# Attention and expert layer on one core: scores of both heads of a pair made at once on halves of TensorE's rows

## The chip, the cores and the metric

The kernel runs on one core of a Trainium2 chip. The metric is the device time of one execution in microseconds (us); the time before the change is the median of three runs, 732.33 us (732.0 to 733.63).

## The reference, cut to what matters

```python
# q, k, v: (8, 8, 576, 64) float32; w_gate (512,), w1 (512, 1024), w2 (1024, 512); capacity 128
q_rot, k_rot = rotate(q), rotate(k)      # halves x1, x2: x1*cos - x2*sin, x1*sin + x2*cos
scores = 0.125 * q_rot @ k_rot.T         # for each batch and head, 576 x 576
attn = exp(scores - max(scores)); attn = attn / (sum(attn) + 1e-9)
x = attn @ v                             # heads side by side: (8, 576, 512)
for b in range(8):
    s = x[b] @ w_gate                    # one score for each token
    top = the 128 tokens with the largest s
    y = relu(x[b, top] @ w1) @ w2
    out[b] = x[b]; out[b, top] += y / (1 + exp(-s[top]))[:, None]
```

Inputs and outputs are float32.

## The kernel before, in words

**Pairs and units.** The work is cut into 32 pairs of heads, four for each batch. A pair has 576 query rows for each of two heads: four tiles of 128 rows for each head (units 0 to 7, the head is the unit's last bit) and the last 64 rows of both heads together (unit 8). Partition p of a main tile holds tokens 4p to 4p+3, so the 64 left over are the "rem" rows.

**From q and k to operands.** `load` brings q, k and v of a pair with DMAs on SyncE (SP). `rotate` makes the rotation on GpSimd (POOL), for the first pair on VectorE (DVE) in two halves. `turn_qk` turns tiles on TensorE (PE) with transposes against an identity and evacuates them from PSUM with ScalarE (ACT) and DVE. The operands of the scores are float32r, and values are split into a high part and a rest. Before the change a stack of 128 rows held one head: `rotate` writes k twice side by side, so that a turned tile has k on both halves of the partitions; q is written as high part and rest side by side. `k1` is the high part of k, `k2` the rest, and one product of 128 rows gives (qh + ql) times kh, a second (qh + ql) times kl: four terms with two products, each for 576 columns in two pieces of 288. That makes 18 transposes a pair: 9 of k in float32 (L418), 9 of q in float32r (L421).

**Scores and softmax.** `unit` (L506) makes the scores of one unit, four matmuls (eight for unit 8) of 288 columns at L519, into one of two score tiles of PSUM (`s_ps`, two banks each). Then DVE takes the row maximum (L532), and ACT the exponential with its sum (L536), which frees the score tile. `turn` (L562) and `turn_rem` (L577, L580) transpose the attention weights, ACT or DVE copy them out (the helper at L232 and L234), and `value` (L612) multiplies them with v: the two heads of a pair stand on the two column halves of the array, 64 columns each. The result is turned back (L633), scaled (L643), and a half row of the output is stored and multiplied with the gate's weights.

**Route and experts.** After the last pair of a batch `route` ranks the 576 gate scores with comparisons on DVE (L752, L760), finds the 128 chosen tokens, gathers them with an indirect DMA, and `experts_of` runs the two layers on them (L872) while the next batch's attention goes on. The experts of the last but one batch are held back to fill the wait for the last batch's route. The expert weights come in 16 DMAs through two staging tiles, and are split by ACT (L933) and POOL (L935), in the first tens of microseconds.

**What sets the order.** Every step is an operation with the engines it can run on, an assumed duration, the operations that it needs and a key. `Order.run` (L61) goes through time once while the program is built and gives each engine that is free the ready operation with the smallest key; that fixes the order on every engine's queue. On the chip each engine works through its queue in that order and waits for what an instruction needs. `KEY` holds the offsets of the keys. PSUM has four more tiles of one bank (`t_ps`) for all else. Steps that cost PE a change of the array's tiling (`mode`) are charged 92 ns in the planner's count.

Of the kernel before, what the change touches and what calls it, by code (L numbers as in the profile page):

```python
# [22 lines left out]
KEY = dict(ahead=5800, lag=5900, rem=0, value=6200, rows=6000, load=117900, rotate=29000, half=7100, gate=29300,  # L23
           route=31600, count=35100, select=13200, turn=53900, step=4600, kstep=1200, hold=3)


class Bank:


    def __init__(self, kind):  # L30
        self.kind, self.slot, self.left, self.end = kind, None, 0, 0.0


class Op:
    __slots__ = ("engines", "fn", "key", "bank", "waits", "outs", "ready", "start", "end", "done", "mode", "seq")


class Order:

# [7 lines left out]
    def op(self, engines, fn, key, after=(), bank=None, mode=0):  # L47

        o = Op()
        o.engines, o.fn, o.key, o.bank, o.mode = engines, fn, key, bank, mode  # L50
# [5 lines left out]
        if bank is not None:  # L56
            bank.left += 1
        self.ops.append(o)
        return o

    def run(self):  # L61
# [18 lines left out]
        while events:  # L80
# [4 lines left out]
            while moved:  # L85
                moved = False
                for e in names:
                    if free[e] > t:
                        continue
                    put, found = [], None  # L90
                    while waiting[e]:
# [4 lines left out]
                        fits = o.ready <= t  # L96
                        if fits and o.bank is not None and o.bank.slot is None:
                            fits = any(a <= t for a, _ in banks[o.bank.kind])
                        if fits:
                            found = o  # L100
                            break
# [3 lines left out]
                    if found is None:  # L105
                        continue
# [11 lines left out]
                    b = o.bank  # L118
                    if b is not None and b.slot is None:
                        ready = min(x for x in banks[b.kind] if x[0] <= t)  # L120
                        banks[b.kind].remove(ready)
                        b.slot = ready[1]
# [4 lines left out]
                    if b is not None:  # L127
                        b.left -= 1
                        b.end = max(b.end, o.end)
                        if not b.left:  # L130
# [33 lines left out]
def attention_moe_kernel(ctx: ExitStack, tc: tile.TileContext, q, k, v, w_gate, w1, w2, rope, outs, cap):  # L164
# [14 lines left out]

    nc = tc.nc  # L180
# [11 lines left out]
    NS = 2 * NT + 1  # L192
# [15 lines left out]
    order = Order({"s": len(s_banks), "t": len(t_banks)})  # L208
# [27 lines left out]
    def bank_of(b):  # L236
        return (s_banks if b.kind == "s" else t_banks)[b.slot]
# [4 lines left out]
    ident_r = sb("ident_r", [P, P], F32R)  # L242
    nc.vector.tensor_copy(ident_r, ident)
    tabs = sb("tabs", [P, 2, NS, D])
# [5 lines left out]
    q_ins = ring("q_in", 2, [P, NS, D])  # L250
    k_ins = ring("k_in", 2, [P, NS, D])
    m2s = ring("m2", 1, [P, NS, D])
    rks = ring("rk", 1, [P, NS, 2, D])
    rqs = ring("rq", 1, [P, NS, 2, D], F32R)
    k1s = ring("k1", 2, [P, 2, KW], F32R)
    k2s = ring("k2", 2, [P, 2, KW], F32R)
    q1s = ring("q1", 2, [P, 2, 512], F32R)
    qrs = ring("qr", 2, [P, 2, 192], F32R)
# [27 lines left out]
    rjs = ring("rj", 1, [P, S], BF16)  # L286
# [3 lines left out]
    for t_ in qrs.tiles:  # L290
        nc.vector.memset(t_.bitcast(F32)[:, 0, 64:192], 0.0)
# [37 lines left out]
    def load(pi):  # L329
# [12 lines left out]
        for n, src, use, late in (("k", k, kin, 0), ("q", q, qin, 1)):  # L342
            dst = use.tile
            dma(n, dst[:, 0:2 * NT, :].rearrange("p (h t) d -> p h t d", h=2), main(src), use, late)
            for h in range(2):
                dma(n, dst[h * 64:h * 64 + 64, 2 * NT, :], rem(src, h), use, late)
# [5 lines left out]
    def rotate(pi):  # L352
# [5 lines left out]
        parts = ((0, NT), (NT, NS)) if first else ((0, NS),)  # L358
        made = {"k": [], "q": []}
# [11 lines left out]
        for s0, s1 in parts:  # L371
            ss, ns = slice(s0, s1), s1 - s0
            cos, sin = tabs[:, 0, ss], tabs[:, 1, ss]
            for name, use, n_ in (("k", kin, 1), ("q", qin, 0)):
                x, m = use.tile[:, ss], m2.tile[:, ss]
                ms = []
                for w in range(2):
                    ws, wo = slice(32 * w, 32 * w + 32), slice(32 - 32 * w, 64 - 32 * w)
                    ms.append(tt(ns * 32, m[:, :, ws], x[:, :, wo], sin[:, :, ws], ALU.mult,
                                 got[name] + m2.before + m2.users + wait, [m2, use]))  # L380
                y = tt(ns * D, x, x, cos, ALU.mult, ms, [use])
                if n_:
                    r = rk.tile[:, ss]
                    yy, mm = (t_.unsqueeze(2).to_broadcast([P, ns, 2, D]) for t_ in (x, m))
                    o = tt(ns * D * 2, r, yy, mm, ALU.add, [y] + rk.before, [use, m2, rk])
                    made["k"].append((s0, o))
                else:
                    hi, lo = rq.tile[:, ss, 0], rq.tile[:, ss, 1]
                    if first:
                        a = tt(ns * D, x, x, m, ALU.add, [y], [use, m2])  # L390
                        h = op({"ACT": act(ns * D)}, lambda hi=hi, x=x: nc.scalar.copy(hi, x), key, [a])
                        rq.by(h)
# [607 lines left out]
```

## Time and profile before

| | before |
|---|---|
| median of three runs | 732.33 us |
| the profiled execution's own time | 733.43 us |
| its span | 731.7 us |
| granted TensorE clock, mean | 0.995 |
| PE busy | 691.9 us, 95% |
| DVE busy | 520.7 us, 71% |
| POOL busy | 490.3 us, 67% |
| ACT busy | 479.6 us, 66% |
| chain that ended last | PE 80%, DVE 6%, issue 5%, ACT 4% |

How to read it: the span runs from the first to the last instruction of the profiled execution, and 1.7 us of its own time lie outside the span. Matmuls are pipelined, so a matmul's recorded duration holds its whole way through the array: what a matmul costs TensorE is the distance to the next start, not its duration. A group's row has its instructions, their summed and mean duration, and behind the bar the idle time of the engine just before them with what ended it.

### The profile page before, as it was taken

What the parts mean: (1) busy time and instruction counts of PE and PEld (TensorE: products, weight loads), DVE (VectorE), ACT (ScalarE), POOL (GpSimd) and SP (SyncE); (2) the same over time, 40 slices, a digit from 0 to 9 for tenths busy, and PEclk for the clock granted to TensorE, in tenths of its full rate; (3) what the DMA queues carried; (4) which work ended last, traced back from release to release, by engine and by line L of the source; (5) the groups of instructions that cost most, each with busy time, mean ns of one, the idle gap of its engine ahead of it and who ended that gap; (6) DMA issues with size and microseconds to landing.
All of it is one profiled execution on the core that took longest, in us unless ns stands there. A gap on an engine that the chain in (4) does not pass through costs nothing.

```text
span 731.7 us, 14829 instructions
## 1 busy us (share of the span) xinstructions
PE 691.9 (95%) x5200; PEld 571.8 (78%) x5200; DVE 520.7 (71%) x1373; ACT 479.6 (66%) x1155; POOL 490.3 (67%) x446
## 2 busy tenths in 40 slices
PE   3789899999999999999999999999999999999986
PEld 2777688788878887888878878788878888788665
DVE  5466568987897478974788658984789747886551
ACT  2777667677777577765777658775777657776311
POOL 3799999878786488773875768864887648741101
PEclk9999999999999999999999999999999999999989
DMA  5334322122212122121312112121221112000100
GB/s 173 108 108 123 94 64 81 49 71 76 80 51 67 33 79 82 50 63 50 96 48 68 50 54 74 49 82 34 78 82 51 49 54 90 17 24 11 50 26 30
DMA packets 55146, 47.95 MB, mean 66 GB/s; under 512 B 17952, under 2 KB 51744, under 8 KB 55072
## 3 DMA queue, kind: packets, MB, share of 16 engines
q1 hardware_dynamic: 53648, 42.23, 19.4%
q0 software_dynamic: 1280, 4.20, 1.7%
q8 instruction: 41, 0.67, 0.4%
q10 hardware_dynamic: 144, 0.59, 0.3%
q14 instruction: 33, 0.27, 0.1%
HBM read 35.45 MB, written 11.53 MB: 64 GB/s over the span
## 4 chain that ended last, share of the span: by engine, by line
PE 80%; DVE 6%; issue 5%; ACT 4%; DMA 2%; POOL 1%; SPq 0%; POOLq 0%; ACTq 0%; DVEq 0%
PE s_ps L519 22%; PE t_ps L612 21%; PE t_ps L562 16%; PE t_ps L872 9%; PE t_ps L418 4%; PE t_ps L421 3%; PE t_ps L633 2%; ACT pab L536 2%; DVE rj L760 2%; PE t_ps L577 2%; DVE rj L752 1%; PE t_ps L580 1%; PE t_ps L891 1%; DMA k_in<-k_dram 1%; ACT pt L232 1%
## 5 line engine op out<-in xcount | busy, mean ns | idle before, releaser
L532 DVE TENSOR_REDUCE nm<-s_ps 128x1 f32<-128x576 f32 x288 | 215.0, 750 | 94.3 <-PE s_ps L519 85.2
L536 ACT ACTIVATE pab<-s_ps,nm 128x576 f32<-128x576 f32 x256 | 192.5, 752 | 38.6 <-DVE nm L532 37.2
L519 PE MATMUL s_ps<-k,q 128*128 128x288 f32 x1024 | 200.0, 318 | 8.7 <-ACT pab L536 8.5
L519 PEld LDWEIGHTS s_ps<-k,q 128*128 128x128 f32 x1024 | 147.2, 191 | 30.1 <-issue 12.8
L232 ACT COPY pt<-t_ps 128x512 f32<-128x512 f32 x214 | 126.4, 591 | 60.7 <-PE t_ps L562 56.9
L562 PE MATMUL t_ps<-ident,pab 128*128 128x128 f32 x1024 | 155.1, 274 | 8.5 <-DVE rj L760 5.8
L612 PE MATMUL t_ps<-pt,vt 128*64 128x320 f32 (+1 forms) x1024 | 139.0, 412 | 0.3 <-ACT pk L232 0.2
L562 PEld LDWEIGHTS t_ps<-ident,pab 128*128 128x128 f32 x1024 | 122.9, 141 | 16.8 <-ACT pt L232 7.2
L366 POOL TENSOR_TENSOR rk<-k_in,m 128x1152 f32<-128x1152 f32 x31 | 82.0, 2646 | 73.0 <-PE t_ps L418 72.7
L612 PEld LDWEIGHTS t_ps<-pt,vt 128*64 128x64 f32 x1024 | 69.0, 136 | 48.2 <-issue 5.0
L234 DVE COPY pt<-t_ps 128x512 f32<-128x512 f32 x74 | 50.7, 685 | 26.6 <-PE t_ps L562 19.7
L232 ACT COPY ot<-t_ps 128x320 f32<-128x320 f32 (+1 forms) x63 | 25.2, 400 | 61.5 <-PE t_ps L612 61.5
L705 POOL TENSOR_TENSOR prod<-x,wg 128x512 f32<-128x512 f32 (+1 forms) x45 | 49.3, 1096 | 19.4 <-DVE gp L710 18.9
L911 POOL DMA_INDIRECT out_dram<-xe,idx x7 | 7.4, 1054 | 80.0 <-DVE xe L907 80.0
L418 PE MATMUL t_ps<-ident,rk 128*128 128x128 f32 x288 | 48.0, 278 | 9.0 <-DVE rk L366 9.0
L366 POOL TENSOR_TENSOR m<-k_in,tabs 128x288 f32<-128x288 f32 x62 | 49.0, 809 | 10.9 <-DVE q_in L366 10.9
L872 PE MATMUL t_ps<-w,ht 128*128 128x512 f32 x192 | 53.3, 419 | 0.0
L536 ACT ACTIVATION_READ_ACCUMULATOR pab<-s_ps,nm 128x1 f32 x256 | 52.9, 207 | 0.0
L872 PE MATMUL t_ps<-w,xt 128*128 128x512 f32 x192 | 49.9, 400 | 0.0
L432 ACT CAST k<-t_ps 128x512 fp32r<-128x512 f32 x64 | 38.0, 596 | 17.8 <-PE t_ps L418 17.0
L366 POOL TENSOR_TENSOR m<-q_in,tabs 128x288 f32<-128x288 f32 x62 | 48.6, 803 | 1.2
L434 DVE TENSOR_TENSOR k<-t_ps,k 128x512 fp32r<-128x512 f32 x64 | 43.4, 680 | 7.3 <-ACT k L432 7.3
(120 smaller groups left out, 1158.2 us busy)
## 6 DMA issues: line engine op xcount, KB each, us to landing
k_in<-k_dram SPq DMA_DIRECT2D x32, 256.0 KB, 2.7
q_in<-q_dram SPq DMA_DIRECT2D x32, 256.0 KB, 2.8
vt<-v_dram SPq DMA_DIRECT2D x32, 256.0 KB, 2.7
out_dram<-x SPq DMA_DIRECT2D x16, 512.0 KB, 3.5
xe<-w_dram SPq DMA_DIRECT2D x8, 256.0 KB, 2.8
row<-w_dram SPq DMA_DIRECT2D x8, 256.0 KB, 2.7
k_in<-k_dram SPq DMA_DIRECT2D x64, 16.0 KB, 2.3
q_in<-q_dram SPq DMA_DIRECT2D x64, 16.0 KB, 2.4
```

Source lines behind the costliest of these rows:

```text
L232: nc.scalar.copy(out, in_)
L234: nc.vector.tensor_copy(out, in_)
L366: lambda: e.tensor_tensor(out, in0, in1, op=alu), key, after)
L418: nc.tensor.transpose(out, rk.tile[:, i].rearrange("p s d -> p (s d)"), ident)
L434: lambda: nc.vector.tensor_tensor(lo, bank_of(b), hi.bitcast(F32), op=ALU.subtract),
L519: nc.tensor.matmul(bank_of(b)[:, n, 0:HALF], lt, rt[:, n * HALF:n * HALF + HALF], start=(i == 0), stop=(i == len(mms) - 1),)
L532: lambda: nc.vector.tensor_reduce(nm.tile[:, u:u + 1], bank_of(b)[:, :, 0:HALF], axis=AX.XY, op=ALU.max, negate=True),
L536: lambda: nc.scalar.activation(dst.rearrange("p (n c) -> p n c", n=2), bank_of(b)[:, :, 0:HALF], AF.Exp, bias=nm.tile[:, u:u + 1], scale=1 ...
L562: nc.tensor.transpose(bank_of(b)[:, kt * P:kt * P + P], src.tile[:, col + kt * P:col + kt * P + P], ident)
L612: nc.tensor.matmul(bank_of(acc)[hp, 0:n], lt, rt, start=kt == 0, stop=kt == NT)
L705: lambda t0=t0, t1=t1, n=n, prod=prod: nc.gpsimd.tensor_tensor(prod.tile[0:n, 0:t1 - t0], x.tile[0:n, t0:t1, :], wg[0:n, cs].unsqueeze(1). ...
L872: nc.tensor.matmul(bank_of(bank), lhs.tile[:, a, c * P:c * P + P], w[w_][:, c, fs], start=(c == 0 and i == 0), stop=(c == n - 1 and i == 2))
```

## The change

q and k are packed by pair: after `rotate` a tile has head 0 on columns 0 to 63 and head 1 on columns 64 to 127, so that turned tiles hold head 0 on partitions 0 to 63 and head 1 on partitions 64 to 127. `turn_qk` then turns 5 tiles of k and 5 of q, all in float32, and splits each into high part and rest (`kh`, `kl`, `qh`, `ql`). `units` makes the scores of one tile of both heads in one operation: twelve matmuls of 288 columns that alternate between partitions 0 to 63 (head 0, score tile a) and 64 to 127 (head 1, score tile b), for the three terms qh kh, qh kl and ql kh; the fourth, ql kl, is left out. Unit 8 keeps all 128 rows (the other head's rows of q are zero) and has 6 matmuls in score tile a. Such an operation needs both score tiles at once. The planner has a new rule: an engine doesn't start an operation when an operation marked urgent (scores, maximum, exponential) can start within 900 ns (`patience`), unless it ends at most 400 ns (`over`) behind that. The keys of all steps, the layout of the rotation's tables and a scratch tile of `route` change too. The rotation of the first pair is no longer cut in two, and its ACT casts (L391) are gone. k's rem rows come with one DMA where there were two.

```diff
+           gate=11700, route=58400, count=35500, select=12400, turn=17500, step=7600, kstep=2700, hold=3,
+           patience=900, over=400)
...
+                        can = o.ready
+                        for b in o.banks:
+                            if b.slot is None:
+                                can = max(can, min((a for a, _ in banks[b.kind]), default=1e12))
+                            elif b.last != e:
+                                can = max(can, b.free)
+                        if can > t:
+                            if o.urgent and can < t + KEY["patience"] and (soon is None or can < soon):
+                                soon = can
+                        elif soon is None or t + o.engines[e][0] <= soon + KEY["over"]:
                             found = o
...
-                        begin += 92.0 * (o.mode != mode) + 70.0 * (t > free[e] + 1)
+                        begin += 97.0 * (o.mode != mode) + 70.0 * (t > free[e] + 1)
...
-    order = Order({"s": len(s_banks), "t": len(t_banks)})
+    order = Order({"a": 1, "b": 1, "t": len(t_banks)})
...
-                    yy, mm = (t_.unsqueeze(2).to_broadcast([P, ns, 2, D]) for t_ in (x, m))
-                    o = tt(ns * D * 2, r, yy, mm, ALU.add, [y] + rk.before, [use, m2, rk])
+            by_head = lambda t_: t_[:, 0:2 * NT].rearrange("p (h t) d -> p h t d", h=2)
+            o = [tt(2 * NT * D, r.tile[:, 0:NT].rearrange("p t h d -> p h t d"), by_head(x), by_head(m), ALU.add,
+                    [y] + r.before, [use, m2, r])]
...
+        kb, ko = turned([(rk, t) for t in range(NT)], base, made["k"][0:1])
+        k_main = split(kb, ko, base, 512, kh.tile[:, REM:REM + 512], kl.tile[:, REM:REM + 512],
+                       lambda: bank_of(kb), 1.0, kh, kl)
...
+        rb, ro = turned([(rk, NT), (rq, NT)], key, made["k"][1:] + made["q"][1:])
...
+        qb, qo = turned([(rq, t) for t in range(NT)], key, made["q"][0:1])
+        q_main = split(qb, qo, key, 512, qh.tile[:, 0:512], ql.tile[:, 0:512],
+                       lambda: bank_of(qb), D ** -0.5, qh, ql)
...
+    STARTS = {(0, 1): 0, (2, 3): 2, (4, 5): 4, (8,): 6, (6, 7): 7}
...
+            bs = tuple(Bank("ab"[i]) for i in range(len(us)))
             mms = []
+            for a, b in ((qh, kh), (qh, kl), (ql, kh)):
+                for n in range(2):
+                    for i, u in enumerate(us):
+                        hp = slice(64 * i, 64 * i + 64) if u < 8 else slice(0, P)
+                        c0, k0 = (u // 2 * P, REM - REM * i) if u < 8 else (512, REM)
+                        mms.append((i, n, a is qh and b is kh, a is ql, a.tile[hp, c0:c0 + P],
+                                    b.tile[hp, k0 + n * HALF:k0 + n * HALF + HALF]))
...
-            o = op(pe(2 * len(mms) * M288), products, key, needs, b)
+            o = op(pe(6 * (M288 + 6 * (len(us) - 1))), products, key, have + room + (q_rem if us[0] == 8 else []), bs,
+                   mode=2 * (len(us) - 1), urgent=True)
```

The lines of the changed program that the rows below name: L428 transposes of k and q, L494 scores, L540, L555 and L558 transposes of the attention weights, L590 value products, L611 transposes of the output, L354 loads, L906 and L911 gate and expert weights, L912 the casts of the expert weights, L438 and L441 the high parts of k and q, L515 the exponentials. Buffers are named with their number: `s_ps0` and `s_ps1` are the two score tiles (a and b).

**TensorE, the second pair's first score units.** Before the change these rows stand there; `q11` and `k11` are the second pair's operands, `vt0` the first pair's v.

```order
L612 MATMUL t_ps3_68<-pk10_110,vr0_99 64x320 x2
L519 MATMUL s_ps1_64<-k11_89,q11_93 128x288 x2
L519 MATMUL s_ps1_64<-k21_91,q11_93 128x288 x2
L519 MATMUL s_ps0_63<-k11_89,q11_93 128x288 x2
L519 MATMUL s_ps0_63<-k21_91,q11_93 128x288 x2
L633 MATMUL t_ps2_67<-ident_69,ot10_112 128x128 x3
```

In the changed program the same place reads so; a group of scores has twelve rows, of which the first two and the last are shown.

```order
L494 MATMUL s_ps0_63<-kh1_87,qh1_91 128x288
L494 MATMUL s_ps1_64<-kh1_87,qh1_91 128x288
...
L494 MATMUL s_ps1_64<-kh1_87,ql1_93 128x288
L540 MATMUL t_ps1_66<-ident_69,pab3_103 128x128 x4
L555 MATMUL t_ps2_67<-ident_69,pab2_102 128x128
L555 MATMUL t_ps2_67<-ident_69,pab3_103 128x128
L558 MATMUL t_ps2_67<-ident_69,pr0_104 128x128 x2
L428 MATMUL t_ps3_68<-ident_69,rk0_84 128x128 x4
L540 MATMUL t_ps0_65<-ident_69,pab0_100 128x128 x4
```

Two units now stand in one block that alternates between both score tiles, and before the next block there are only transposes, 16 here: the block behind them needs both tiles again.

**SyncE, the loads at the start.** Before the change the expert weights' first DMA (`xe0`) stands behind v of the third pair (`vt2`) and a reload of `k_in0`.

```order
L338 DMA vr1_100<-v_dram 64x64 x2
L338 DMA vt2_98<-v_dram 128x2x256
L338 DMA vr2_101<-v_dram 64x64 x2
L338 DMA k_in0_83<-k_dram 128x2x256
L338 DMA k_in0_83<-k_dram 64x64 x2
L927 DMA wg_77<-w_gate_dram 128x512
L932 DMA xe0_128<-w1_dram 128x512
```

In the changed program it follows the loads of the first two pairs.

```order
L354 DMA vr1_98<-v_dram 64x64 x2
L906 DMA wg_75<-w_gate_dram 128x512
L911 DMA xe0_126<-w1_dram 128x512
L911 DMA row0_128<-w1_dram 128x512
L354 DMA k_in0_81<-k_dram 128x2x256
```

Six DMAs have moved behind the first two weight loads, and k's rem rows are one DMA each.

**ScalarE, the first exponentials.** Before the change one weight cast (`w1_0`) stands ahead of them.

```order
L478 ACTIVATE qr0_94<-t_ps3_68 128x2x64
L448 ACTIVATE q10_92<-t_ps0_65 128x512
L933 CAST w1_0_142<-xe0_128 128x512
L536 ACTIVATE pab0_102,sums0_115<-s_ps0_63,nm0_118 128x576
L536 ACTIVATE pab0_102,sums0_115<-s_ps1_64,nm0_118 128x576
```

In the changed program two do.

```order
L441 ACTIVATE qh0_90<-t_ps2_67 128x128
L912 CAST w1_0_139<-xe0_126 128x512
L912 CAST w1_0_139<-row0_128 128x512
L515 ACTIVATE pab0_100,sums0_113<-s_ps0_63,nm0_116 128x576
L515 ACTIVATE pab0_100,sums0_113<-s_ps1_64,nm0_116 128x576
```

So the first exponentials wait for two weight loads instead of one, and these loads are issued earlier.

More of the change, by code (lines that the diff above doesn't have):

```diff
@@ L20 @@
 EPS = 1e-9
-KEY = dict(ahead=5800, lag=5900, rem=0, value=6200, rows=6000, load=117900, rotate=29000, half=7100, gate=29300,
-           route=31600, count=35100, select=13200, turn=53900, step=4600, kstep=1200, hold=3)
+KEY = dict(ahead=8500, lag=13000, rem=400, value=4300, rows=18600, load=22300, rotate=115700, half=2500,
+           gate=11700, route=58400, count=35500, select=12400, turn=17500, step=7600, kstep=2700, hold=3,
+           patience=900, over=400)
 class Bank:
     def __init__(self, kind):
-        self.kind, self.slot, self.left, self.end = kind, None, 0, 0.0
+        self.kind, self.slot, self.left, self.end, self.last, self.free = kind, None, 0, 0.0, None, 0.0
 class Op:
-    __slots__ = ("engines", "fn", "key", "bank", "waits", "outs", "ready", "start", "end", "done", "mode", "seq")
+    __slots__ = ("engines", "fn", "key", "banks", "waits", "outs", "ready", "start", "end", "done", "mode", "seq", "urgent")
 class Order:
@@ L55, in op @@
             a.outs.append(o)
-        if bank is not None:
-            bank.left += 1
+        for b in banks:
+            b.left += 1
         self.ops.append(o)
@@ L126, in run @@
                     heapq.heappush(events, free[e])
-                    if b is not None:
+                    for b in o.banks:
                         b.left -= 1
                         b.end = max(b.end, o.end)
+                        b.last, b.free = e, b.end + self.SEM
+                        heapq.heappush(events, b.free)
                         if not b.left:
@@ L420, in q_turn, with turned @@
-        def q_turn(out, i):
-            nc.tensor.transpose(out, rq.tile[:, i].rearrange("p s d -> p (s d)"), ident_r)
-        def k_main(h, key):
+        def turned(tiles, key, needs):
             b = Bank("t")
             def turns():
-                for t in range(NT):
-                    k_turn(bank_of(b)[:, t * P:t * P + P], h * NT + t)
-            hi, lo = k1.tile[:, h, REM:REM + 512], k2.tile[:, h, REM:REM + 512]
-            o = op(pe(4 * T32), turns, key, by("k", h * NT), b)
-            c = op({"ACT": act(512)}, lambda: nc.scalar.copy(hi, bank_of(b)), key, [o] + k1.before, b)
-            d = op({"DVE": dve(512)},
-                   lambda: nc.vector.tensor_tensor(lo, bank_of(b), hi.bitcast(F32), op=ALU.subtract),
-                   key, [c] + k2.before, b)
-            rk.by(o), k1.by(c, d), k2.by(d)
-            have[f"k{h}"] += [c, d]
@@ L484, in turn_qk @@
-        step = KEY["kstep"]
-        k_main(0, base)
-        q_main(0, base + step)
-        rems(base + 2 * step)
-        k_main(1, base + 3 * step)
-        q_main(1, base + 4 * step)
-        stacks[pi] = (q1, qr, k1, k2, have)
+                for i, (r, t) in enumerate(tiles):
+                    nc.tensor.transpose(
+                        bank_of(b)[:, i * P:i * P + P], r.tile[:, t].rearrange("p h d -> p (h d)"), ident)
+            o = op(pe(len(tiles) * T32), turns, key, needs + kh.before + kl.before + qh.before + ql.before, b)
```

248 lines of the change are left out of this document (108 added, 140 removed).

## The prediction

> **What bounds the kernel now.** I read the page's busy times first, then the stages, TensorE's waits, and a stretch of TensorE's timeline for prices.
>
> ```profile
> PE 691.9 (95%) x5200; PEld 571.8 (78%) x5200; DVE 520.7 (71%) x1373; ACT 479.6 (66%) x1155; POOL 490.3 (67%) x446
> ```
>
> Busy TensorE may only be a pipeline full of latency, so the stages must confirm it. Two successive batches in the middle (columns: window, its length, then busy time of PE, PEld, DVE, ACT, POOL with instructions, TensorE's clock, DMA):
>
> ```profile
> 203.30:289.10 85.80, 84.74 (x653) 70.47 (x651) 63.54 (x166) 59.03 (x144) 60.46 (x54) 1.00 0.21 63
> 289.10:374.80 85.70, 84.63 (x652) 70.38 (x651) 63.46 (x166) 58.93 (x144) 60.41 (x54) 1.00 0.21 62
> ```
>
> A batch takes 85.7 us, and TensorE is idle for 1.1 of them, at full clock; DVE has 22 us to spare, ACT 27, POOL 25. What TensorE waits for in the whole span (sum, times, longest):
>
> ```profile
> PE t_ps L418 <- DVE rk L366: 9.0, 2, 7.9
> PE s_ps L519 <- ACT pab L536: 8.6, 13, 4.0
> PE t_ps L562 <- DVE rj L760: 5.8, 7, 0.8
> ...
> PE t_ps L562 <- ACT pab L536: 2.7, 3, 1.1
> ```
>
> The 9.0 are the first rotation, the 5.8 the route of each batch. TensorE's work sets the time, so I price the change as work of TensorE, then ask which wait takes the place of that work. A stretch of TensorE (start, length, operation):
>
> ```profile
> 300.32 0.60 PE L562 MATMUL t_ps<-ident,pab 128*128 128x128 f32 x4
> 300.85 2.37 PE L612 MATMUL t_ps<-pt,vt 128*64 128x320 f32 x16
> 303.06 0.71 PE L612 MATMUL t_ps<-pk,vr 128*64 128x320 f32 x4
> 303.69 0.80 PE L519 MATMUL s_ps<-k,q 128*128 128x288 f32 x4
> 304.33 0.60 PE L562 MATMUL t_ps<-ident,pab 128*128 128x128 f32 x4
> 304.68 0.77 PE L519 MATMUL s_ps<-k,q 128*128 128x288 f32 x4
> 305.29 0.60 PE L562 MATMUL t_ps<-ident,pab 128*128 128x128 f32 x4
> 305.73 0.60 PE L844 MATMUL t_ps<-ident,xe 128*128 128x128 f32 x4
> 306.17 0.60 PE L418 MATMUL t_ps<-ident,rk 128*128 128x128 f32 x4
> 306.52 0.54 PE L421 MATMUL t_ps<-ident_r,rq 128*128 128x128 f32 x4
> 306.99 0.80 PE L519 MATMUL s_ps<-k,q 128*128 128x288 f32 x4
> 307.62 0.60 PE L562 MATMUL t_ps<-ident,pab 128*128 128x128 f32 x4
> 307.98 1.30 PE L519 MATMUL s_ps<-k,qr 128*128 128x288 f32 x8
> 309.11 0.38 PE L577 MATMUL t_ps<-ident,pab 128*128 128x128 f32 x2
> ```
>
> Starts give the prices. Four float32 transposes take 0.44 us (305.29 to 305.73 to 306.17): 0.109 each. Eight score matmuls run from 307.62 + 0.44 = 308.06 to 309.11: 0.132 each. Four float32r transposes run from 306.17 + 0.44 = 306.61 to 306.99: 0.095 each.
>
> The same rows price a change of the array's tiling. Transposes end at 300.32 + 0.44 = 300.76, the value product on column halves starts at 300.85: 0.09 us of nothing. On the way out its last two pairs need 2 x 0.27 from 303.06, so 303.60, and scores start at 303.69: 0.09 again. And the first unit behind it takes 0.64 (303.69 to 304.33) where one behind transposes takes 305.29 - (304.33 + 0.44) = 0.52: 0.11 us in which the first weights load with nothing over them.
>
> **The change part by part.** Counts and durations of the groups:
>
> ```profile
> L519 PE MATMUL s_ps<-k,q 128*128 128x288 f32 x1024 | 200.0, 318 | 8.7 <-ACT pab L536 8.5 <-DVE k L472 0.2
> L519 PE MATMUL s_ps<-k,qr 128*128 128x288 f32 x256 | 41.8, 305 | 0.2 <-ACT pab L536 0.2
> L612 PE MATMUL t_ps<-pt,vt 128*64 128x320 f32 x512 | 76.7, 439 | 0.3 <-ACT pk L232 0.2
> L612 PE MATMUL t_ps<-pt,vt 128*64 128x256 f32 x512 | 62.3, 385 | 0.0
> L418 PE MATMUL t_ps<-ident,rk 128*128 128x128 f32 x288 | 48.0, 278 | 9.0 <-DVE rk L366 9.0
> L421 PE MATMUL t_ps<-ident_r,rq 128*128 128x128 f32 x288 | 42.4, 262 | 3.3 <-DVE rq L366 3.3
> ```
>
> *Scores.* Before: 1280 matmuls x 0.132 = 169.0 us. After, for each pair, 4 groups of 6 slots with two matmuls each (one a half of rows), and 6 full matmuls for unit 8. What is a slot worth? No row shows halves of rows; the nearest are the halves of columns. There 64 columns more make a matmul 439 - 385 = 54 ns longer, 0.84 ns a column, so 320 columns stream for 0.27 us; yet 16 matmuls start within 2.21 us (300.85 to 303.06), 0.14 each. So two run at once, at almost no cost. Bounds for a slot of scores: 0.132 (the second matmul free) and 0.264 (one after the other). I take 0.139, near the value product's behaviour. Sum: 768 x 0.139 + 192 x 0.132 = 132.1, a gain of 36.9 us.
>
> The Trainium skill's "TensorE: Matmul & The Clock Gate" (Measured speedup vs the span model) has four row tiles 3.07 times as fast, 77% of four. By that rule a slot is 0.264 / 1.53 = 0.172, an estimate, and the gain on scores only 11.6.
>
> *Transposes of q and k.* Before 288 x 0.109 + 288 x 0.095 = 58.8 us, after 320 x 0.109 = 34.9: a gain of 23.9.
>
> *Changes of tiling.* Every group on row halves stands between work in another tiling. The order of the changed program has 327 changes on TensorE, the order before 128 (64 value products, in and out). Into a score group: 0.09 + 0.11 = 0.20, 128 times, 25.6 us. Into a value product: 0.09 + about 0.05 for its half as wide weights, 64 times, 9.0. Back to transposes or full matmuls: 0.09 and a first load that these rows bound by 0 and 0.11, I take 0.07, 135 times, 21.6. Together 56, before 20 by the same prices (64 x 0.14 and 64 x 0.18): a loss of 36. This eats the whole gain on scores.
>
> *The start.* The first scores of before stand behind the rotation, and then behind a weight load:
>
> ```profile
> 16.16 2.25 PE L519 MATMUL s_ps<-k,q 128*128 128x288 f32 x8
> ...
> 20.98 0.62 ACT L933 CAST w<-xe 128x512 fp32r<-128x512 f32 x1 [3.98 <-DMA xe<-w_dram]
> 21.50 0.73 ACT L536 ACTIVATE pab<-s_ps,nm 128x576 f32<-128x576 f32 x1
> ...
> 22.14 0.19 ACT L536 ACTIVATION_READ_ACCUMULATOR pab<-s_ps,nm 128x1 f32 x1
> 22.23 0.73 ACT L536 ACTIVATE pab<-s_ps,nm 128x576 f32<-128x576 f32 x1
> 22.38 0.85 PE L519 MATMUL s_ps<-k,q 128*128 128x288 f32 x2 [3.97 <-ACT pab L536]
> ```
>
> The rotation itself, two of its sums on DVE in that timeline:
>
> ```profile
> 7.07 0.69 DVE L366 TENSOR_TENSOR rk<-k_in,m 128x512 f32<-128x512 f32 x1
> ...
> 11.70 0.82 DVE L366 TENSOR_TENSOR rk<-k_in,m 128x640 f32<-128x640 f32 x1
> ```
>
> The first rotation falls from 4608 to 3712 elements a partition, at 0.13 us for 128 (the two rows) 0.9 us, and has seven instructions fewer, each with some 0.17 of its own (0.69 less four times 0.13) that partly overlaps, some 0.6: 1.5 us earlier. The weight DMA is issued eight issues earlier (six moved behind, two fewer rem loads), so I drop its stall of 3.97 although two casts now stand ahead of the exponentials; if it stays, 4 us come back.
>
> *The new wait.* A score group needs both score tiles. All of TensorE's queue stands behind it, transposes and value products included, and DVE and ACT wait for those. How soon are both tiles free? The lone unit at the end shows the steps:
>
> ```profile
> 680.16 0.69 PE L519 MATMUL s_ps<-k,q 128*128 128x288 f32 x4
> ...
> 680.95 0.76 DVE L532 TENSOR_REDUCE nm<-s_ps 128x1 f32<-128x576 f32 x1 [3.05 <-PE s_ps L519]
> 681.74 0.74 ACT L536 ACTIVATE pab<-s_ps,nm 128x576 f32<-128x576 f32 x1 [2.20 <-DVE nm L532]
> ```
>
> Five slots 0.70 and a last matmul through the array 0.29, 0.10 to the maximum, 0.76 for it, 0.03 to the exponential, 0.73 until the second one starts (21.50 to 22.23), 0.83 until its sum is read (21.50 to 22.33), 0.05 to TensorE (22.38), 0.11 first load: 3.6 us from group to group; 2.9 and 2.8 into and out of unit 8, which needs one tile. I priced the order's rows between all 160 score groups. Where experts run (a batch of 20 intervals, 81 us) the two-tile intervals are 3.8 us or longer. In the first 12 pairs many are 2.9 to 3.3, as in the second order shown in the change. What falls short adds up to 13 us without any queueing on DVE and ACT, 20 us if each loop loses 0.2, 33 at 0.4, 51 at 0.6. Copies of 0.6 to 0.7 us stand in those queues, and the planner lets one overrun an urgent step by at most 0.4; I take the middle of that, 0.2, so 20 us, 18 of them in the first 12 pairs. TensorE's waits for exponentials of before, 8.6 + 2.7 = 11.3 us, are replaced by these.
>
> *At nothing:* POOL's rotation falls from 5184 to 3712 elements a partition for each pair, DVE takes more copies and ACT fewer; all had over 20 us of a batch to spare. Expert matmuls that the order moves behind the last scores are moved work, and the tail behind them stays.
>
> *The sum:* 733.4 (the profiled execution) - 36.9 - 23.9 + 36 - 1.5 + 20 - 11.3 = 715.8 us. That execution lies 1.1 us above the median of 732.3; the terms are rounded to more than that, so I say 716 beside the median.
>
> **The rivals.** *A, better than forecast:* slot 0.132 (-5.4) and no queueing (-7): about 703 us. For it speaks the spare time of DVE and ACT, against it that both work through their queues in order.
>
> *B, the score loop becomes the bound:* each loop loses more than the planner thinks, since a change of tiling costs TensorE 0.16 to 0.20 where the planner charges 0.097, so that its order is late everywhere. At 0.4 us a loop 729 us, at 0.6 747; it turns into a loss from 0.45 on. For it: DVE, busy for 63.5 us of a batch now, has as much to do in a shorter one, and three steps in a row go through two queues. Against: with experts the intervals have 0.2 us and more of slack, and a TensorE that is late makes the loops less tight.
>
> *C, slower: the halves' weight loads run one after the other.* A load took 0.11 us above; two in turn are 0.21 to 0.22 a slot, more than the stream of 288 columns, and 768 slots x 0.075 are 58 us: about 773. It becomes a loss from 0.16 a slot on (16 us over 768 slots). For it: each half brings weights of 128 columns. Against: the value product's two half loads hide under a slot. The skill's page named above says (LDWEIGHTS) that a load's time goes by its columns and not by its rows; by that rule half a load costs a whole one, some 107 ns by its formula, an estimate, and no run here shows two at once on row halves. Its 3.07 would give 741 by this sum, and of C's chance I give 0.05 to a slot near that. That the halves don't run at once at all is the end of this rival, over 800 us.
>
> **How the numbers follow.** The forecast, slot 0.132 to 0.145 and 0.1 to 0.35 us a loop, has 0.53 and reaches from 704 to 727; A 0.15, below it; B 0.18, from 727 to 747, of which 0.10 is still faster, 0.02 the same; C 0.12; 0.02 is left for the rest, half on each side. A measurement of this kernel tells 0.2% from no change, 1.5 us: faster below 730.8, slower above 733.8. Faster 0.53 + 0.15 + 0.10 + 0.01 = 0.79, same 0.02, slower 0.06 + 0.12 + 0.01 = 0.19. For 8 in 10 the range goes from 699, in A, to 739, in B, and leaves out C.
>
> **What would show it.** Slots: starts of matmuls in a score group 0.139 apart by twos; at 0.17 or 0.21 C holds. Tiling: 0.09 and 0.11 ahead of each group, 0.09 and some 0.07 behind. Loops: TensorE's waits for the exponentials near 20 us, nearly all before 260 us; over 35 means B. A batch in the middle near 83 us where it was 85.7. The start: first scores before 15 us, and no wait of 4 us behind them. I would be wrong most of all if a middle batch took 85 us or more.

## The result and the profile after

The changed kernel takes 707.25 us (median of 4 runs, 705.83 to 709.07) where the kernel before takes 732.17 beside it: a ratio of 0.9657, 95% interval 0.963 to 0.9684. The profiled execution took 706.6 us, its span is 704.9. Against the profiled execution of before (733.4, span 731.7) that is 26.8 us less.

The busy times from the page of the changed kernel:

```profile
PE 665.3 (94%) x5392; PEld 507.1 (72%) x5392; DVE 528.4 (75%) x1373; ACT 421.3 (60%) x1047; POOL 399.3 (57%) x481
```

TensorE lost 26.6 us of busy time, the span 26.8. Two batches in the middle (window, length, then the busy time of each engine with its instructions, TensorE's clock, DMA):

```profile
316.13:398.33 82.20, 81.68 (x676) 62.60 (x675) 65.30 (x167) 50.93 (x130) 48.76 (x58) 1.00 0.23 65
398.33:480.53 82.20, 81.68 (x677) 62.61 (x675) 65.31 (x167) 50.93 (x130) 48.79 (x58) 1.00 0.23 66
```

A batch takes 82.2 us instead of 85.7, and TensorE is idle for 0.5 of them: there is no new wait in it. The score loop has come nearer, though: of the chain that ended last, followed back through what released each step, DVE now has 16% where it had 6, and the maxima (L511) alone 5%.

```profile
PE 72%; DVE 16%; issue 6%; ACT 4%; SPq 1%; DMA 1%; POOL 0%; POOLq 0%; DVEq 0%; ACTq 0%
```

What TensorE waits for in the whole span (waits under 0.15 us are not listed):

```profile
PE t_ps L540 <- ACT pab L515: 8.5, 7, 2.6
PE t_ps L428 <- DVE rk L384: 8.1, 1, 8.1
PE t_ps L540 <- ACT pt L248: 3.0, 3, 1.0
PE s_ps L494 <- ACT pr L515: 2.1, 5, 0.8
...
PE s_ps L494 <- ACT pab L515: 1.7, 2, 0.9
```

The waits for exponentials (the rows that end in L515) are 8.5 + 2.1 + 1.7 = 12.3 us, about what the 11.3 of before were; 11.0 of them lie before 260 us. A stretch of TensorE's timeline (start, length, operation):

```profile
301.03 0.53 PE L494 MATMUL s_ps<-kh,qh 64*128 64x288 f32 x4
301.40 0.43 PE L494 MATMUL s_ps<-kl,qh 64*128 64x288 f32 x4
301.67 0.42 PE L494 MATMUL s_ps<-kh,ql 64*128 64x288 f32 x4
302.02 0.66 PE L540 MATMUL t_ps<-ident,pab 128*128 128x128 f32 x4
302.51 0.38 PE L555 MATMUL t_ps<-ident,pab 128*128 128x128 f32 x2
302.73 0.60 PE L540 MATMUL t_ps<-ident,pab 128*128 128x128 f32 x4
...
304.77 0.60 PE L540 MATMUL t_ps<-ident,pab 128*128 128x128 f32 x4
305.30 0.48 PE L494 MATMUL s_ps<-kh,qh 64*128 64x288 f32 x2
```

Four matmuls are two slots of two: 301.40 to 301.67 is 0.27, so a slot is about 0.132 (a single record starts 0.131 to 0.134 us behind the pair ahead of it, and its partner 4 to 6 ns after it). The second head is free. The edges: transposes end at 304.77 + 0.44 = 305.21 and scores start at 305.30, 0.09; the first slot is 0.10 longer than the next ones (301.03 to 301.40 is 0.37 for two); six slots, 0.79, and that 0.10 end at 301.92, and the transposes start at 302.02, 0.10 by these rounded figures and 0.09 in most groups; the first four of these take 0.49 instead of 0.44. So it costs 0.20 into a group and 0.145 out of it.

The start:

```profile
13.02 1.00 PE L494 MATMUL s_ps<-kh,qh 64*128 64x288 f32 x4 [0.26 <-ACT qh L441]
...
15.80 0.62 ACT L912 CAST w<-xe 128x512 fp32r<-128x512 f32 x1 [2.49 <-DMA xe<-w_dram]
...
17.02 0.74 ACT L515 ACTIVATE pab<-s_ps,nm 128x576 f32<-128x576 f32 x1
...
17.90 1.11 PE L540 MATMUL t_ps<-ident,pab 128*128 128x128 f32 x4 [2.63 <-ACT pab L515]
```

The first scores start 3.1 us earlier than before. The weight load still holds up ACT, and so TensorE, but by 2.5 to 2.6 us and no longer by 4.0.

### The profile page after: what moved, and what is told of

Its sections match the earlier page's. It is cut to its first block, busy times and chain, and to the rows that moved or that the text cites. A ratio compares the mean times of both kernels' runs of the same rounds, so it can differ in the third digit from the quotient of the medians.

```text
span 704.9 us, 15143 instructions
## 1 busy us (share of the span) xinstructions
PE 665.3 (94%) x5392; PEld 507.1 (72%) x5392; DVE 528.4 (75%) x1373; ACT 421.3 (60%) x1047; POOL 399.3 (57%) x481
## 4 chain that ended last, share of the span: by engine, by line
PE 72%; DVE 16%; issue 6%; ACT 4%; SPq 1%; DMA 1%; POOL 0%; POOLq 0%; DVEq 0%; ACTq 0%
PE t_ps L590 21%; PE s_ps L494 19%; PE t_ps L540 15%; PE t_ps L851 7%; DVE nm L511 5%; PE t_ps L428 4%; DVE sel L731 3%; DVE pt L250 2%; PE t_ps L611 2%; DVE sel L738 1%; PE t_ps L555 1%; SPq L354 1%; ACT pab L515 1%; ACT pt L248 1%; PE t_ps L558 1%
## 5 line engine op out<-in xcount | busy, mean ns | idle before, releaser
L511 DVE TENSOR_REDUCE nm<-s_ps 128x1 f32<-128x576 f32 x288 | 205.4, 750 | 87.4 <-PE s_ps L494 84.1
L515 ACT ACTIVATE pab<-s_ps,nm 128x576 f32<-128x576 f32 x256 | 187.9, 741 | 67.9 <-DVE nm L511 67.2
L540 PE MATMUL t_ps<-ident,pab 128*128 128x128 f32 x1024 | 153.2, 279 | 13.3 <-ACT pab L515 8.5
L540 PEld LDWEIGHTS t_ps<-ident,pab 128*128 128x128 f32 x1024 | 115.3, 141 | 37.4 <-ACT pab L515 13.1
L590 PE MATMUL t_ps<-pt,vt 128*64 128x320 f32 (+1 forms) x1024 | 138.3, 412 | 0.2
L384 POOL TENSOR_TENSOR rk<-k_in,m 128x512 f32<-128x512 f32 (+1 forms) x62 | 53.4, 869 | 126.0 <-PE t_ps L428 125.7
L590 PEld LDWEIGHTS t_ps<-pt,vt 128*64 128x64 f32 x1024 | 67.8, 136 | 49.0 <-issue 7.3
L494 PE MATMUL s_ps<-kh,qh 64*128 64x288 f32 (+1 forms) x576 | 87.8, 347 | 4.2 <-ACT pr L515 2.1
L494 PEld LDWEIGHTS s_ps<-kh,qh 64*128 64x128 f32 (+1 forms) x576 | 50.1, 186 | 44.5 <-ACT pab L515 18.1
L494 PE MATMUL s_ps<-kl,qh 64*128 64x288 f32 (+1 forms) x576 | 70.9, 294 | 0.0
L494 PE MATMUL s_ps<-kh,ql 64*128 64x288 f32 (+1 forms) x576 | 70.9, 293 | 0.0
L384 POOL TENSOR_TENSOR rq<-q_in,m 64x64 f32<-64x64 f32 (+1 forms) x93 | 58.1, 639 | 16.1 <-PE t_ps L428 13.2
L384 POOL TENSOR_TENSOR m<-k_in,tabs 128x320 f32<-128x320 f32 x62 | 52.6, 868 | 9.7 <-DVE rq L384 7.6
L494 PEld LDWEIGHTS s_ps<-kl,qh 64*128 64x128 f32 (+1 forms) x576 | 53.8, 187 | 0.2 <-DVE kl L439 0.2
L494 PEld LDWEIGHTS s_ps<-kh,ql 64*128 64x128 f32 (+1 forms) x576 | 53.9, 187 | 0.0
L515 ACT ACTIVATION_READ_ACCUMULATOR pab<-s_ps,nm 128x1 f32 x256 | 51.4, 201 | 0.0
L384 POOL TENSOR_TENSOR k_in<-k_in,tabs 128x640 f32<-128x640 f32 x31 | 48.2, 1555 | 2.3
```

Of the source, the lines that this page charges most:

```text
L384: lambda: e.tensor_tensor(out, in0, in1, op=alu), key, after)
L494: nc.tensor.matmul(bank_of(bs[i])[:, n, 0:HALF], lt, rt, start=first, stop=last)
L511: lambda: nc.vector.tensor_reduce(nm.tile[:, u:u + 1], bank_of(b)[:, :, 0:HALF], axis=AX.XY, op=ALU.max, negate=True),
L515: lambda: nc.scalar.activation(dst.rearrange("p (n c) -> p n c", n=2), bank_of(b)[:, :, 0:HALF], AF.Exp, bias=nm.tile[:, u:u + 1], scale=1 ...
L540: nc.tensor.transpose(bank_of(b)[:, kt * P:kt * P + P], src.tile[:, col + kt * P:col + kt * P + P], ident)
L590: nc.tensor.matmul(bank_of(acc)[hp, 0:n], lt, rt, start=kt == 0, stop=kt == NT)
```

## Experiments

My theory from the two profiles: TensorE's work sets the time, and it fell by 42 us in the scores (a slot of two for the price of one, three terms) and 21 in the transposes, of which the changes of tiling took some 36 back; the order only has to keep TensorE fed. Two rivals: the halves are not what counts, or the score loop (scores, maximum, exponential) through VectorE and ScalarE sets the time and the new order is what made room for it.

In the first six runs, down to the doubled transposes, the planner does not see the edit, so that all queues keep the order of the changed kernel; in the five behind them it makes another order.

**The halves apart.** The matmuls of a group sorted by head:

```diff
-                for i, n, first, last, lt, rt in mms:
+                for i, n, first, last, lt, rt in sorted(mms, key=lambda m: m[0]):
```

> The twelve matmuls of a two-tile score group are issued sorted by head (all six of rows 0 to 63, then all six of rows 64 to 127) instead of alternating. Nothing else moves. Theory (the second half is free only because its neighbour in the queue is on the other half; a slot of two takes 0.132 us): a group now takes about 11 slots of 0.132 instead of 6, so +0.66 to +0.79 us for each of 128 groups, 84 to 101 us, a total near 790 to 808. Rival (the time of a group comes from something else, such as its operands or its exit, and alternation does not matter): within 5 us of the changed kernel's 707.

Measured: 747.27 us (ratio to before 1.0214, 1.019 to 1.0237), 40 more than the changed kernel: neither. One group in TensorE's timeline:

```profile
302.68 0.52 PE L494 MATMUL s_ps<-kh,qh 64*128 64x288 f32 x2
303.04 0.29 PE L494 MATMUL s_ps<-kl,qh 64*128 64x288 f32 x1
303.05 0.39 PE L494 MATMUL s_ps<-kh,qh 64*128 64x288 f32 x1
303.17 0.29 PE L494 MATMUL s_ps<-kl,qh 64*128 64x288 f32 x1
303.28 0.28 PE L494 MATMUL s_ps<-kh,qh 64*128 64x288 f32 x1
303.30 0.29 PE L494 MATMUL s_ps<-kh,ql 64*128 64x288 f32 x1
303.41 0.29 PE L494 MATMUL s_ps<-kl,qh 64*128 64x288 f32 x1
303.43 0.29 PE L494 MATMUL s_ps<-kh,ql 64*128 64x288 f32 x1
303.54 0.29 PE L494 MATMUL s_ps<-kl,qh 64*128 64x288 f32 x1
303.67 0.42 PE L494 MATMUL s_ps<-kh,ql 64*128 64x288 f32 x2
304.02 1.66 PE L851 MATMUL t_ps<-w,xt 128*128 128x512 f32 x6
```

The kh,qh at 303.05 is the second head's first matmul, seventh in the queue; it starts 7 ns behind the first head's third, and the fourth to sixth start after it (303.17, 303.30, 303.43). TensorE let the other half's work pass what stood ahead of it, so four of a head's six slots still overlap with the other head's. This corrects the description of the kernel, by which every engine works through its queue in order: for matmuls on the two row halves TensorE does not. The group takes 1.34 us instead of 0.99: 128 x 0.35 = 45 us of work, and 40 in the time.

**The halves apart, with an instruction on whole rows between them.**

```diff
+                    if i_ == 0 and len(us) == 2:
+                        nc.tensor.transpose(bank_of(bs[0])[:, 1, 320:448], ident, ident)
```

> The matmuls of a two-tile group sorted by head, with the extra whole-row transpose between the two heads' six. To be compared with the kernel that has this transpose ahead of the group (723.6). Theory (with the halves only sorted, TensorE began the second head's matmuls 0.37 us after the first's, past three that stood ahead of them; an instruction on whole rows between stops that): six more slots of 0.132 and two more tiling changes of together 0.296, 128 x 1.09 = 139 us more, near 862. Rival (the overlap goes on past it): 723.6 + 38 + 40, near 801.

Measured: 864.08 us (1.1809, 1.1759 to 1.186), 140.4 above the kernel with that transpose ahead of the group, where 139 was expected. That kernel's group (first fence) and this one's (second), by TensorE's timeline:

```profile
288.12 0.27 PE L494 MATMUL s_ps<-ident 128*128 128x128 f32 x1
288.32 0.40 PE L498 MATMUL s_ps<-kh,qh 64*128 64x288 f32 x2
288.56 0.29 PE L498 MATMUL s_ps<-kl,qh 64*128 64x288 f32 x2
288.69 0.30 PE L498 MATMUL s_ps<-kh,ql 64*128 64x288 f32 x2
...
289.08 0.29 PE L498 MATMUL s_ps<-kh,ql 64*128 64x288 f32 x2
```

```profile
300.24 0.53 PE L496 MATMUL s_ps<-kh,qh 64*128 64x288 f32 x2
300.62 0.42 PE L496 MATMUL s_ps<-kl,qh 64*128 64x288 f32 x2
300.88 0.43 PE L496 MATMUL s_ps<-kh,ql 64*128 64x288 f32 x2
301.24 0.33 PE L498 MATMUL s_ps<-ident 128*128 128x128 f32 x1
301.49 0.53 PE L496 MATMUL s_ps<-kh,qh 64*128 64x288 f32 x2
```

In the first an x2 is one slot (0.13 from line to line), in the second it is two (0.26). That two heads share a slot is worth six slots of 0.132 a group, 101 us in all; the rival that the halves don't matter is out.

**Two more changes of tiling a group.** The same transpose between the two column pieces of a group, and, to compare, ahead of it (there the last two lines stand above the loop, under `if len(us) == 2`):

```diff
+                for n_ in range(2):
+                    for i, n, first, last, lt, rt in mms:
+                        if n == n_:
+                            nc.tensor.matmul(bank_of(bs[i])[:, n, 0:HALF], lt, rt, start=first, stop=last)
+                    if n_ == 0 and len(us) == 2:
+                        nc.tensor.transpose(bank_of(bs[0])[:, 1, 320:448], ident, ident)
```

> Each two-tile score group is issued column piece by column piece, and one extra transpose of a constant (128x128, whole rows, into unused columns of the tile) stands between the two pieces: two more changes of tiling in each of 128 groups. To be compared with the next run, which has the same extra transpose ahead of the group. Theory (a change into a score group costs 0.197 us beside the instructions, out of it 0.146): this run is 128 x 0.343 = 44 us longer than the next, near 765. Rival (what was read at the edges of the groups is their semaphores and not the change of tiling): within 10 us of the next run.

> As the run before it, with the extra transpose ahead of the group, where as a rule other transposes stand already, so that no tiling change is added. Theory: only the transpose's own 0.109 us for each of 128 groups, 14 us more than the changed kernel: near 721. Rival (an extra instruction at the group's head delays both heads' exponentials by more than itself): 730 or more.

Measured: 761.55 us between (1.0409, 1.0388 to 1.043) and 723.64 ahead (0.9891, 0.9871 to 0.9911). The transpose alone costs 16.4, expected 14; the two changes of tiling 37.9, expected 44: net 0.296 us for a way in and out instead of 0.343. The starts around the transpose are those of the 0.343 (from the last slot to the transpose 0.222, to the next slot 0.259, to the one after it 0.239). The comparison itself was not clean: in 27 of the 128 groups a value product stood directly ahead, so that the transpose ahead adds a change of tiling too (354 in that order, not 327). By the starts, these 27 x 0.09 = 2.4 us of the 44 are in both kernels (the 16.4 lie above the 14 by as much), and TensorE's waits fell by 3.9, from 31.0 to 27.1: that leaves 37.7, about what was measured. Tiling changes are a real cost, and some of any cost is taken out of waits.

**A fourth term.** The product of ql and kl added to the two-tile groups:

```diff
-            for a, b in ((qh, kh), (qh, kl), (ql, kh)):
+            terms = ((qh, kh), (qh, kl), (ql, kh)) + (((ql, kl),) if us[0] < 8 else ())
+            for a, b in terms:
```

> The product of the two remainders, ql by kl, is computed too in the two-tile groups: 8 slots in each instead of 6. Theory (scores on halves save only as much as the third-term form saves, since the tiling changes give back most of it): 128 x 2 x 0.132 = 34 us more than the changed kernel, near 741, slower than the kernel before. Rival (TensorE has slack inside the score loop, which hides part of it): 715 to 730.

Measured: 736.62 us (1.007, 1.0053 to 1.0087): 29.4 more than the changed kernel, and slower than before. In the trace the starts of score matmuls take 34.0 us more, as expected, and TensorE's waits are 29.7 instead of 32.4. Between the two expectations, nearer the first: row halves with four terms, as many as before, lose in this order.

**The transposes.** The eight main transposes of q and k made twice, 18 a pair as before:

```diff
-                for i, (r, t) in enumerate(tiles):
+                for i, (r, t) in list(enumerate(tiles)) * (len(tiles) // 2):
```

> The eight main transposes of q and k of each pair are made twice, so that a pair has 18 again as before the change; order and all else as in the changed kernel. Theory (TensorE sets the time, and what it does less there is won in full): 256 x 0.109 = 28 us more, near 735. Rival (part of the transposes lies in waits for the exponentials or for the loads): 715 to 728.

Measured: 726.74 us (0.9928, 0.9902 to 0.9955), 19.5 more, in the rival's stretch. The distances between transposes grew by 28.8 us, and these waits of TensorE fell:

```profile
PE t_ps L540 <- ACT pab L515: 7.1, 6, 1.8
PE t_ps L540 <- ACT pt L248: 2.5, 3, 1.0
...
PE s_ps L494 <- ACT pr L515: 0.8, 1, 0.8
```

All listed waits together are 27.5 us instead of 32.4. Another 2.7 us came out of waits too short for the list: in 22 places scores of unit 8 follow a transpose, and the distances from its start to theirs come to 1.4 us instead of 4.1. Work added between two score groups gives the loop time, so added work cost some 70 to 85% of itself (19.5 of 28.8 here, 29.4 of 34.0 for the fourth term).

**The loop.** The kernel without the row maximum (the bias of the exponential is a constant zero):

```diff
-            m = op({"DVE": dve(S)},
-                   lambda: nc.vector.tensor_reduce(
-                       nm.tile[:, u:u + 1], bank_of(b)[:, :, 0:HALF], axis=AX.XY, op=ALU.max, negate=True),
-                   key, [o] + nm.before, b, urgent=True)
...
-                   key, [m] + into.before + sums.before, b, urgent=True)
+                   key, [o] + into.before + sums.before, b, urgent=True)
```

> This kernel leaves out the row maximum: the bias of the exponential is a constant zero, the exponential follows the scores directly, and VectorE loses 256 reductions. What it gains bounds what the loop through VectorE costs the changed kernel. Theory (the waits for exponentials and maxima are about 12 us in all, most at the start and the first pairs, and TensorE sets the rest): 694 to 703. Rival (the score loop of about 4 us still sets the rate and its cost is hidden in how the work is ordered): 690 or less.

Measured: 699.04 us (0.9545, 0.9525 to 0.9564), 8.2 less, as the theory had it. All of TensorE's waits come to 24.9 us, those for exponentials to the 2.9 of this row:

```profile
PE t_ps L538 <- ACT pab L513: 2.9, 2, 2.6
```

But 8 us is no strict bound on what VectorE's part of the loop costs, since the planner makes another order, with 351 changes of tiling instead of 327. Pair 12 (counted from 0) starts at 232.6 instead of 245.3 us, 12.7 earlier; a batch in the middle takes 82.9 instead of 82.2. So the loop costs the changed kernel up to some 13 us at the start, and in the middle, where VectorE with 170 us less work made nothing faster, it does not set the time.

**The order.** First without the planner's rule by which an engine waits for an urgent operation:

```diff
-                            if o.urgent and can < t + KEY["patience"] and (soon is None or can < soon):
+                            if False and o.urgent and can < t + KEY["patience"] and (soon is None or can < soon):
```

> The planner's rule that an engine waits for an urgent operation that will be ready soon is taken out; values, operations and the rest of the planner are those of the changed kernel. Theory (waits for the exponentials stay small because the queueing of the score loop sits in intervals that have slack, whoever orders them): within 5 us of 707. Rival (the rule is what keeps the score loop short; without it scores, maxima and exponentials stand behind other work): the queueing per loop goes from about 0.4 us to 0.8 or more and the total to 720 to 745.

Measured: 745.92 us (1.0187, 1.0168 to 1.0206): 38.7 more, and slower than before. Here my theory falls. TensorE's waits:

```profile
PE t_ps L540 <- ACT pab L515: 19.5, 19, 2.8
...
PE t_ps L540 <- DVE x L621: 6.1, 6, 2.5
PE s_ps L494 <- ACT pab L515: 5.0, 12, 0.9
PE t_ps L540 <- DVE pt L250: 3.9, 11, 0.6
```

All of them come to 56.7 us instead of 32.4. The loop itself is hardly longer: from the first score of a two-tile group until both its tiles are read it takes 3.93 us in the mean instead of 3.87, and 3.78 in the median of both. The rival had the queueing per loop double, and it did not. What grew is the time from free score tiles to the next group's first score, from 0.44 us in the mean to 0.68, and from 70 to 109 us in sum. One such place, where the exponential's sum is read at 54.33:

```profile
54.13 0.20 ACT L515 ACTIVATION_READ_ACCUMULATOR pab<-s_ps,nm 128x1 f32 x1
54.24 1.95 PE L590 MATMUL t_ps<-pt,vt 128*64 128x256 f32 x16
...
56.02 0.60 PE L590 MATMUL t_ps<-pk,vr 128*64 128x256 f32 x4
...
56.55 0.54 PE L494 MATMUL s_ps<-kh,qh 64*128 64x288 f32 x4
```

TensorE has begun a value product 0.09 us before the tiles are free, and the scores start 2.2 us late. Without the rule 53 two-tile groups stand directly behind a value product, with it 27; the delays of all score groups that follow a value product come to 72 us instead of 30. Pair 12 starts at 271.4 instead of 245.3, so 26 of the 42 us between the two profiled executions are lost in the first 12 pairs; in the middle a batch takes 86.0 instead of 82.2 (in pairs 16 to 19, as an exception, 82.4).

Then with the values of the kernel before and the rule kept:

```diff
-KEY = dict(ahead=8500, lag=13000, rem=400, value=4300, rows=18600, load=22300, rotate=115700, half=2500,
-           gate=11700, route=58400, count=35500, select=12400, turn=17500, step=7600, kstep=2700, hold=3,
+KEY = dict(ahead=5800, lag=5900, rem=0, value=6200, rows=6000, load=117900, rotate=29000, half=7100, gate=29300,
+           route=31600, count=35100, select=13200, turn=53900, step=4600, kstep=1200, hold=3,
```

> The planner's key values are those of the kernel before, with the waiting rule and its patience kept. Theory (the gain is that of the work of TensorE, 668 us before and 642 after, and the order only has to keep it fed): 705 to 715. Rival (the new values are needed, since at the start and at the pairs' boundaries the order decides): over 720, with waits for exponentials or for loads above 25 us.

Measured: 745.37 us (1.0177, 1.0156 to 1.0198), the rival's side. The waits are 57.4 us, among them

```profile
PE t_ps L540 <- ACT pab L515: 13.2, 14, 2.4
PE t_ps L540 <- DVE sel L738: 10.9, 6, 2.1
```

so that TensorE waits for exponentials and, new in this order, for the route's selections on VectorE. Here too the loop is not longer (3.83 us in the mean), and the delays of the score groups come to 114 us instead of 70.

Third, the planner with the prices that the trace gave, and without its extra price for a slot of two:

```diff
-                        begin += 97.0 * (o.mode != mode) + 70.0 * (t > free[e] + 1)
+                        begin += (196.0 if o.mode == 2 else 146.0) * (o.mode != mode) + 70.0 * (t > free[e] + 1)
...
-            o = op(pe(6 * (M288 + 6 * (len(us) - 1))), products, key, have + room + (q_rem if us[0] == 8 else []), bs,
+            o = op(pe(6 * M288), products, key, have + room + (q_rem if us[0] == 8 else []), bs,
```

> The planner is given measured prices: 196 ns for a change into a score group and 146 out of it or between other tilings, in place of 97 for any, and no extra price per slot of two. Theory (the order already groups the work as well as the score tiles allow, 327 changes): within 4 us of 707. Rival (the planner changes tiling too often because it thinks it cheap): some 30 to 60 fewer changes, 5 to 10 us faster, 697 to 702.

Measured: 720.33 us (0.9848, 0.9831 to 0.9864), 13.1 more: both expectations missed. The order has 344 changes of tiling instead of 327, and the waits on the score tiles grew:

```profile
PE s_ps L494 <- ACT pab L515: 9.8, 19, 1.0
PE t_ps L540 <- ACT pab L515: 9.6, 8, 2.3
```

All waits are 38.0 us instead of 32.4, and 17 changes at about 0.17 are 3 us more. A likely reason is that the due times suit the planner's own prices, and that a truer price alone moves the order away from them; no run here shows it. None of these three orders is better than the changed kernel's.

Last, the rule in the kernel before, its scores, maxima and exponentials marked urgent:

```diff
+                            if o.urgent and can < t + KEY["patience"] and (soon is None or can < soon):
+                                soon = can
+                        elif soon is None or t + o.engines[e][0] <= soon + KEY["over"]:
...
-            o = op(pe(2 * len(mms) * M288), products, key, needs, b)
+            o = op(pe(2 * len(mms) * M288), products, key, needs, b, urgent=True)
```

> The kernel before, with the planner's waiting rule (same patience and same excess) and its scores, maxima and exponentials marked urgent; its values, transposes and scores are its own. Theory (the rule is worth 39 us only where a two-tile group needs both score tiles free at once; with one-tile groups the loops of two tiles overlap and nothing is gained): 728 to 740. Rival (the rule is a gain of its own, and packing and halves are worth little): 715 or less.

Measured: 734.45 us (10 runs; 1.004, 1.0026 to 1.0053), as the theory had it. The rule is no gain by itself; with two-tile groups, taking it out costs 39 us. No run chose the due times anew for either planner, so how much of the 39 us is the rule's alone, and how much the due times' that go with it, stays open.

## Why the forecast held, and where its terms were off

Forecast 716 us beside the median, measured 707.25, within the forecast's own stretch of 704 to 727 and nearer to rival A's 703. The path was right: TensorE's work bounds both kernels, and the tiling eats most of what the halves give. The two terms in which A differs came out as A had them (slot 0.132; 12.3 us of waits where A has 13). The sum against the profiled execution, 715.8 for 706.6, is off by 9.2 us: scores 5.4 and waits 7.7 better than forecast, the start 1.6 better, transposes 2.8 worse, and 2.7 worse spread over the rest. By steps:

- *Scores, -36.9:* the mechanism held, the size was off. The slot is 0.132 and not 0.139, so 960 x 0.132 = 126.7 us, a gain of 42.3. I took 0.139, by the value product; but a slot of two takes 0.276 us there (2.21 for eight) where 320 columns at 0.84 ns stream for 0.269, 3% more, which would have been 0.136. The lower bound was right. The estimate from the Trainium skill's "TensorE: Matmul & The Clock Gate" (Measured speedup vs the span model), whose 3.07 is for four row tiles, was 0.172; here two halves together take as long as one full matmul, which is twice as fast as one half after the other, and the measurement decides. Rival C is out: a load of 64 rows takes 0.184 us in the median, about as long as one of 128 rows with 0.188, but the two of a slot start 4 ns apart, and slots follow each other after 0.132.
- *Transposes, -23.9:* 21.1. Those of float32r start 0.085 apart in the trace before, not 0.095; the rest of that reading belongs to the step into the score group behind them. Doubling the transposes showed that their removal is worth less than their own time, since part of it comes back as waiting.
- *Tiling, +36:* 0.20 in and 0.145 out give 128 x 0.20 + 135 x 0.145 + 64 x 0.14 = 54 us with the forecast's 0.14 for value products, and 57 when the changed order is priced row by row; less the 20 of before, 34 to 37. (The sum took 0.18 for a way out before and 0.16 after, not quite the same price; that is 1.3 us.) Scores and tiling together are worth only 5 to 8 us; three terms (34.0 us of slots) make the difference between that and a loss.
- *Start, -1.5:* 3.1; 0.6 of it because the first rotation begins at 5.51 us instead of 6.08, which the sum left out. Of the weight load's stall, which I dropped, 2.5 stayed.
- *New waits, +20 for the 11.3 of before:* 12.3 measured, 11.0 of them before 260 us, where the forecast expected them. This is the term that was sized wrong, and not because the loops were quick. From the first score to both tiles read the forecast's steps give 3.44 us; the trace has 3.44 as the least, 3.78 in the median and 3.87 in the mean, so a loop loses 0.34 to 0.43, not 0.2, and my table had 33 us for 0.4. But a delay counts only where the interval behind it is short. After 260 us 33 two-tile loops took over 3.9 us, and TensorE stood idle behind them for 0.7 us in all. Why the table overstates the early pairs too is not shown.
- *Rivals:* B's time was nearer than its 0.18 says: without the waiting rule the kernel takes 746 us, about what B gave for 0.6 us a loop, and with the old values 745. But B's mechanism is not what these runs show, so the agreement is luck. Their loops are not longer (3.93 and 3.83 us), and the order without the rule has 320 changes of tiling, seven fewer; its score groups start late, behind other work of TensorE. What the forecast had no term for is that delay: I had judged the order only by the rule's limit of 0.4.

Start and waits together came to +0.6 us by what the other terms leave, forecast +7.2; 12.3 - 11.3 - 3.1 = -2.1 of it is placed, 2.7 are spread over other waits and edges. What the runs don't settle is why the measured prices make the planner's order worse; that it adds 17 changes and waits on the score tiles is shown, which due time does it is not.

## What to carry to other kernels

Price a packed form by its slots, its changes of tiling and the terms that it drops together: here the halves alone paid for little more than their edges, and the gain came from dropped work. Where two tiles must be free at once, the order of the queues is worth as much as the change itself (39 us for the rule, 38 for the values, a gain of 25), so move work and order together and measure the order apart. Ask then how soon a group starts after its tiles are free, and not only how long its loop takes. Work added back to the bounding engine cost some 70 to 85% of its time here, and most of the rest came out of waits: less work between two groups leaves less room for the loop.

## What the chip showed that was not expected

- Matmuls on row halves need not alternate in the queue. Sorted by head, the second head's first matmul started 0.37 us after the first head's, ahead of three that stood before it; a single 128x128 transpose between them stopped this (864 us, where 801 was expected if the overlap had gone on).
- Two score matmuls of 64 rows by 288 columns took the time of one, 0.132 us, with starts 4 to 6 ns apart, although each weight load takes 0.184 us.
- The way out of a tiling costs the next transposes too: the first of them is followed after 0.165 us instead of 0.109, besides the 0.09 of nothing ahead of it.
